# Full and 64-row matmuls chosen piece by piece in a fused attention and FFN kernel, with a new order of TensorE's work

## The chip, the cores and the metric

The kernel runs on one core of a Trainium2 chip. The core has a matrix engine (TensorE, PE in the profile; its weight loads stand as PEld), three engines for elementwise work (VectorE or DVE, ScalarE or ACT, GpSimd or POOL), and SyncE (SP), which here only issues DMA transfers. The metric is the device time of one execution in microseconds, lower being better. The time before is 522.56 us, the median of three runs between 522.38 and 522.78 us.

## The reference

Attention with mixed heads, and behind it a feed-forward network with a squared ReLU:

```python
scores = scale * np.matmul(q, k.transpose(0, 1, 3, 2))        # (8, 12, 448, 448)
scores = np.einsum('bhij,hg->bgij', scores, w_pre)            # heads mixed
attn = np.exp(scores - np.max(scores, axis=-1, keepdims=True))
attn = attn / (np.sum(attn, axis=-1, keepdims=True) + 1e-09)
attn = np.einsum('bhij,hg->bgij', attn, w_post)               # heads mixed again
attn_out = np.matmul(attn, v)                                 # (8, 12, 448, 64)
x = attn_out.transpose(0, 2, 1, 3).reshape(3584, 768)
h = np.maximum(x @ w_in, 0.0)                                 # w_in (768, 2048)
out = h * h @ w_out                                           # w_out (2048, 768)
```

There are 8 batches, 12 heads, 448 positions and a head size of 64. Inputs and output are float32; the products run in bfloat16.

## The kernel before

Work is cut into units, each a short run of matmuls on TensorE. For each batch there are these kinds:

- `tr` (L718): q and k are transposed, 28 small matmuls a unit.
- `qk` (L864): the scores of two heads (or of four half tiles) for a tile of up to 128 query rows. ACT or DVE evicts the result from PSUM to the buffer `stage`, which has two slots, one per query tile. SP then issues relays: DMA transfers that move ten query rows of all heads at a time from `stage` to the ring `dring` (L910). A tile's evictions wait until the relays of the tile two before it have landed.
- `dir` (L815): for the first 22 chunks of batch 0 the scores are made without that relay.
- `pre` (L933): two chunks of ten rows are mixed over heads. ACT takes the exponential and the row sums (L950), DVE the reciprocal (L964), and POOL (DVE in the first chunks) scales the mixing weights and a rest of the exponentials with it (L971, L986).
- `post` (L1016, L1031): the second mixing, fourteen matmuls of 60 columns for two chunks, evicted to `a2t` in two halves.
- `av` (L1097): the product with v, evicted to `xt`, the FFN's input in transposed form.
- `h` (L1148, L1176): the FFN's first product. The 2048 inner features are 16 blocks of 128; a block needs six steps of 128 input features. In batches 0, 1 and 7 a block covers half of the batch's positions (220 or 228), otherwise all 448.
- `o` (L1242, L1293): the second product, for a tile of 128 positions and two halves of 384 output columns, sixteen steps each. Evictions go to `osb`, and POOL issues two stores for each tile (L1325).

A block of the first product is evicted with a ReLU on ACT or DVE (L1204, L1205) and squared on DVE (L1214).

The first product exists in two forms. The full form uses all 128 rows of the array: six matmuls a block (`emit_F1_full`, L1148, used for batches 0 and 1). The other uses 64-row tiles: two blocks are made together, every step is cut into two matmuls of 64 rows that run side by side in the upper and the lower half of the array, each for another block and into another PSUM bank; then the halves change places (`emit_F1`, L1176). A pair of blocks is two units of twelve matmuls, and both blocks are finished only at the end of the second. The second product is in 64-row tiles too (`emit_F2`, L1293), each of its four units sixteen matmuls, save for the last two tiles of the last batch (`emit_last`, L1242).

All eight PSUM banks are handed out by a planner, which walks through a model of the kernel when the program is built. Ten streams hold the units in their own sequence: 0 `tr`, 1 `qk`, 2 `pre`, 3 `post`, 4 `av`, 5 `dir`, 6 and 7 `h`, 8 and 9 `o`. A string of digits, `ORDER`, says from which stream TensorE takes its next unit. For the other engines the planner takes what its model has ready first, and a `FLEX` task goes to ACT or DVE, whichever would end it sooner in the model. So TensorE's order is written out, and the order on the other engines, the waits and the banks follow from it through the planner's costs. A unit whose bank is still to be evicted waits, and on every engine what is behind a waiting instruction waits too.

## Time and profile before

| what | value |
|---|---|
| time, median of three runs | 522.56 us (522.38 to 522.78) |
| profiled execution, first to last instruction | 522.5 us |
| PE busy | 508.7 us, 97%, 9,477 matmuls |
| ACT busy | 432.9 us, 83% |
| DVE busy | 402.8 us, 77% |
| POOL busy | 264.7 us, 51% |
| DMA moved | 72.36 MB, mean 138 GB/s |

No other time of the profiled execution is listed than its span; the median of the runs lies 0.06 us above it. The profile comes as a page with busy times, strips of 40 slices and groups of instructions, and as answers to questions: tables by stage, the chain of work that ended last (followed back from the last instruction to what released it), the waits, and the instructions in order of time. In such a row a number in square brackets is the idle time of the engine just before, with what ended it.

### The profile page before, as it was taken

Reading aid. Unit: us, or ns where it says so; the run is one execution under the profiler, and the core shown is the slowest. Engines: PE = TensorE matmul, PEld = TensorE weight load, DVE = VectorE, ACT = ScalarE, POOL = GpSimd, SP = SyncE. Lnnn points to the kernel's source line nnn. Section 1 sums busy time; section 2 is a strip of 40 time slices with the busy share of each in tenths; the row PEclk is TensorE's granted clock in tenths of the full one; section 3 lists DMA queues with packets and bytes.
Section 4 is the critical chain, followed back from the end, with each engine's and each line's share of the span. In section 5 each row is a group of like instructions: output and inputs, shape, how many; then the busy total and the mean of one; then the engine's idle time right before and its main releaser. Section 6 shows DMA issues by size and latency. Waiting matters only on the chain.

```text
span 522.5 us, 23103 instructions
## 1 busy us (share of the span) xinstructions
PE 508.7 (97%) x9477; PEld 320.4 (61%) x9477; DVE 402.8 (77%) x1038; ACT 432.9 (83%) x1243; POOL 264.7 (51%) x571
## 2 busy tenths in 40 slices
PE   8999999899989999999999999999999999999997
PEld 3455677567757665557546665566555665568874
DVE  8988878779969879977798868986797857955440
ACT  4899989889989889988998898999788899867421
POOL 9926556534753477335672486435654354243000
PEclk9999999999999999999999999999999999999999
DMA  8999989945995489646994689537985557451013
GB/s 113 194 228 181 215 166 182 191 93 114 170 192 131 108 163 180 146 94 155 177 183 86 138 174 191 125 70 159 175 141 114 132 129 136 85 128 53 3 24 99
DMA packets 83024, 72.36 MB, mean 138 GB/s; under 512 B 7160, under 2 KB 80424, under 8 KB 82920
## 3 DMA queue, kind: packets, MB, share of 16 engines
q0 software_dynamic: 37632, 33.83, 39.8%
q1 hardware_dynamic: 45000, 36.86, 29.2%
q8 instruction: 76, 1.25, 1.0%
q14 instruction: 28, 0.23, 0.1%
q10 hardware_dynamic: 288, 0.20, 0.1%
HBM read 47.27 MB, written 11.01 MB: 112 GB/s over the span
## 4 chain that ended last, share of the span: by engine, by line
PE 81%; DVE 7%; ACT 5%; DMA 5%; issue 1%; POOL 0%; SPq 0%; DVEq 0%
PE ps L1293 25%; PE ps L1176 18%; PE ps L933 6%; PE ps L1016 6%; PE ps L1097 6%; PE ps L864 5%; PE ps L815 5%; DMA dring<-stage 5%; PE ps L1148 4%; ACT pring L950 3%; DVE stage L479 2%; PE ps L1242 2%; PE ps L718 2%; PE ps L591 1%; DVE qkt L479 1%
## 5 line engine op out<-in xcount | busy, mean ns | idle before, releaser
L950 ACT ACTIVATE pring<-ps 128x448 bf16<-128x448 f32 x360 | 192.0, 560 | 12.9 <-PE ps L933 11.8
L1293 PE MATMUL ps<-w_out_sb,h2t 64*128 64x384 bf16 x1664 | 151.6, 323 | 2.3 <-issue 1.7
L971 POOL TENSOR_TENSOR wk2s<-wk2b,rinv 128x120 bf16<-128x120 bf16 (+1 forms) x179 | 70.5, 394 | 142.3 <-DVE rinv L964 141.2
L479 DVE CAST a2t<-ps 128x420 bf16<-128x420 f32 (+1 forms) x202 | 122.2, 640 | 15.5 <-PE ps L1031 14.4
L1176 PE MATMUL ps<-xt,w_in_sb 64*128 64x448 bf16 (+2 forms) x1344 | 120.7, 323 | 0.1
L478 ACT ACTIVATE stage<-ps 128x448 bf16<-128x448 f32 (+1 forms) x195 | 101.2, 556 | 14.9 <-PE ps L864 11.9
L478 ACT ACTIVATE a2t<-ps 128x420 bf16<-128x420 f32 (+1 forms) x166 | 99.7, 655 | 15.5 <-PE ps L1031 15.3
L479 DVE CAST stage<-ps 128x448 bf16<-128x448 f32 (+1 forms) x165 | 98.9, 615 | 16.8 <-PE ps L864 13.0
L1293 PEld LDWEIGHTS ps<-w_out_sb,h2t 64*128 64x128 bf16 x1664 | 77.5, 94 | 52.0 <-issue 4.0
L1176 PEld LDWEIGHTS ps<-xt,w_in_sb 64*128 64x128 bf16 x1344 | 61.7, 94 | 40.0 <-PE ps L933 2.0
L1325 POOL DMA_DIRECT2D out_dram<-osb x52 | 33.6, 652 | 100.8 <-ACT pring L950 39.6
L950 ACT ACTIVATION_READ_ACCUMULATOR pring<-ps 128x1 f32 x360 | 81.2, 226 | 0.0
L986 POOL TENSOR_TENSOR ptail<-pring,rinv 128x128 bf16<-128x128 bf16 x171 | 70.2, 411 | 0.0
L1016 PEld LDWEIGHTS ps<-wk2s,pring 60*128 60x128 bf16 x2160 | 47.7, 94 | 25.9 <-DVE stage L479 2.3
L1205 DVE TENSOR_SCALAR h1t<-ps 128x448 bf16<-128x448 f32 (+2 forms) x99 | 46.9, 482 | 14.4 <-PE ps L1176 11.3
L1016 PE MATMUL ps<-wk2s,pring 60*128 60x60 bf16 x2160 | 55.1, 187 | 2.3 <-DVE stage L479 1.1
L1214 DVE TENSOR_TENSOR h2t<-h1t 128x448 bf16<-128x448 bf16 (+2 forms) x176 | 55.5, 345 | 2.1 <-ACT h1t L1204 1.5
L933 PE MATMUL ps<-dring,wk 64*64 64x448 bf16 (+1 forms) x676 | 52.6, 363 | 1.4 <-ACT stage L478 0.8
L964 DVE RECIPROCAL rinv<-rowsum 128x2 f32<-128x2 f32 (+1 forms) x184 | 29.0, 157 | 31.5 <-ACT pring L950 30.7
L864 PE MATMUL ps<-qkt 64*128 64x448 bf16 (+1 forms) x360 | 50.3, 353 | 1.5 <-DVE stage L479 0.6
L1204 ACT ACTIVATE h1t<-ps 128x448 bf16<-128x448 f32 (+2 forms) x77 | 35.0, 461 | 14.4 <-PE ps L1176 12.6
L1097 PEld LDWEIGHTS ps<-a2t,vraw 128*64 128x64 bf16 x960 | 38.5, 109 | 6.0 <-ACT osb L478 2.4
(60 smaller groups left out, 536.8 us busy)
## 6 DMA issues: line engine op xcount, KB each, us to landing
dring<-stage SPq DMA_DIRECT2D x309, 105.0 KB
out_dram<-osb POOLq DMA_DIRECT2D x52, 192.0 KB, 3.9
vraw<-in_v_dram POOLq DMA_DIRECT2D x48, 128.0 KB
qraw<-in_q_dram POOLq DMA_DIRECT2D x48, 112.0 KB, 5.2
kraw<-in_k_dram POOLq DMA_DIRECT2D x48, 112.0 KB, 4.9
w_in_sb<-in_moe_w_in_dram POOLq DMA_DIRECT2D x8, 384.0 KB, 19.6
w_out_sb<-in_moe_w_out_dram POOLq DMA_DIRECT2D x8, 384.0 KB, 16.0
dring<-stage SPq DMA_DIRECT2D x30, 42.0 KB
```

Of the source, the lines that this page charges most:

```text
L478: return eng.activation(o, i_, AF.Copy)
L479: return eng.tensor_copy(o, i_)
L864: r_ = eng.matmul(ps[y * w:(y + 1) * w, g.banks[x], 0:S], qkt[r0:r0 + 64, pb, p + y, 0, i0:i0 + w], qkt[r0:r0 + 64, pb, p + y, 1, :], star ...
L933: r_ = eng.matmul(ps[64 * y:64 * y + 64, gr.banks[x], 0:S], wk1[64 * x:64 * x + 64 - R0 * x, :], dring[64 * x:64 * x + 64 - R0 * x, (g0 + ...
L950: return eng.activation(pring[:, pr, 0:S], ps[:, gr.banks[x], 0:S], AF.Exp, accum_out=rowsum[:, pr, :])
L971: return eng.tensor_tensor(wk2s[:, p0:p0 + n, :], i0.to_broadcast([128, n, PR]), rinv[:, p0:p0 + n, :].to_broadcast([128, n, PR]), ALU.mult)
L986: return eng.tensor_tensor(ptail[:, p0 // 2, :, :], pring[:, p0:p0 + 2, 0:PJ], rinv[:, p0:p0 + 2, :].to_broadcast([128, 2, PJ]), ALU.mult)
L1016: r_ = eng.matmul(ps[:, gr.banks[x], o0:o0 + PR], pring[64 * x:64 * x + PR, pr + y, (2 * k + 1) * PJ:(2 * k + 3) * PJ], wk2s[64 * x:64 * x ...
L1097: r_ = eng.matmul(po, vraw[:, h, sl, :], m, start=(k == 0), stop=(k == NS))
L1176: r_ = eng.matmul(ps[:, g.banks[x], 0:n], w_in_sb[64 * y:64 * y + 64, ft, t * 128:(t + 1) * 128], xt[64 * y:64 * y + 64, ft, c0:c1], start ...
L1214: return eng.tensor_tensor(h2t[:, t16, o0:o0 + n], h1t[:, s, 0:n], h1t[:, s, 0:n], ALU.mult)
L1293: r_ = eng.matmul(ps[:, g.banks[hh], 0:FH], h2t[64 * y:64 * y + 64, t16, col:col + 128], w_out_sb[64 * y:64 * y + 64, t16, hh * FH:(hh + 1 ...
```

## The change

Both products get a flag for each piece. `F1_FULL` has one digit for each of the 88 pairs of blocks: 16 each for batches 0, 1 and 7, 8 each for batches 2 to 6. `F2_FULL` has one for each of 32 places (four to a batch; tiles count from 0). A pair with a 1 is made in the full form: two units of six matmuls, each with a bank of its own, so that the first block can be evicted while the second is made. With a 0 it is made in 64-row tiles as before. A tile of the second product with a 1 has its two halves made one after the other in full matmuls. The one string `ORDER` is replaced by another; it differs from the 38th unit on. Batches 0 and 1 stay full, which they were. Beyond them 9 pairs become full in batches 3, 4 and 5 (two, two and five), 14 of the 16 pairs of batch 7, and its tiles 0 and 1.

```diff
 ORDER = (
-    "0011055055105510551555511155555553115550013555555553135002555555335555335531002555112551"
+    "0011055055105510551555511155555553315555150031555551355555020555533553355522003555111551"
...
 )
+F1_FULL = "1111111111111111111111111111111100000000000001010000001100101111000000001011111011111111"
+F2_FULL = "00000000000000000000000000001100"
...
-        def emit_F1(b, parts, t16, s_F):
+        def emit_F1(b, parts, t16, s_F, full):
             c0, c1 = cols_of(parts[0])[0], cols_of(parts[-1])[1]
             n = c1 - c0
-            g = _Group(2)
-            before = None
+            gs = [_Group(1), _Group(1)] if full else [_Group(2)]
+            ins = ([t for part in parts for t in xtev[(b, part)]]
+                   + w_of[(0, t16 * NWP // NFFT)])
+            ths = []
             for ph in range(2):
                 def fn_h(eng, en, ph=ph):
                     r_ = None
                     for ft in range(NFT):
+                        if full:
+                            t = t16 + ph
+                            r_ = eng.matmul(ps[:, gs[ph].banks[0], 0:n],
+                                            w_in_sb[:, ft, t * 128:(t + 1) * 128],
+                                            xt[:, ft, c0:c1],
+                                            start=(ft == 0), stop=(ft == NFT - 1))
+                            continue
                         for y in range(2):
...
+                before = [] if full else ths[:]
+                t_h = unit(s_F, "h%d_%d_%d_%d" % (b, c0, t16, ph), fn_h, ins + before,
+                           NFT * (n / 2.4 + (2.5 if full else 4.3)), "full" if full else "row",
+                           gs[ph] if full else gs[0], NFT if full else 2 * NFT)
+                t_h.sync = before
+                ths.append(t_h)
...
             for x in range(2):
-                after_F1(b, parts, t16 + x, t_h, c0, n, g, x)
+                after_F1(b, parts, t16 + x, ths[x if full else 1], c0, n,
+                         gs[x] if full else gs[0], 0 if full else x)
...
-            g = _Group(2)
+            full = F2_FULL[4 * b + tile] == "1"
+            gs = [_Group(1), _Group(1)] if full else [_Group(2)]
...
                         for t16 in range(q0, q0 + nk):
+                            if full:
+                                r_ = eng.matmul(
+                                    ps[:, gs[ph].banks[0], 0:FH],
+                                    h2t[:, t16, col:col + 128],
+                                    w_out_sb[:, t16, ph * FH:(ph + 1) * FH],
+                                    start=(t16 == 0), stop=(t16 == NFFT - 1))
+                                continue
...
                 for t16 in range(0, NFFT, 2):
-                    if b < 2:
-                        for t in range(2):
-                            emit_F1_full(b, parts, t16 + t, s_F1[t16 // 2 % 2])
-                    else:
-                        emit_F1(b, parts, t16, s_F1[t16 // 2 % 2])
+                    emit_F1(b, parts, t16, s_F1[t16 // 2 % 2], F1_FULL[n_f] == "1")
+                    n_f += 1
```

How the change moves instructions is shown at three places, in rows that give line, operation, operands, shape and count. Lines of the changed kernel stand two or more higher or lower than those before.

Place A is on PE, at about 56 us of the profile before: the scores (`qk`, written to `ps` from `qkt`) of batch 1's second query tile, between blocks of batch 0's first product (`ps<-xt,w_in_sb`) and the last `pre` units of batch 0 (`ps<-dring,wk`). Before:

```order
L864 MATMUL ps<-qkt 128x448 x4
L1148 MATMUL ps<-xt,w_in_sb 128x220 x12
L864 MATMUL ps<-qkt 128x448 x2
L1016 MATMUL ps<-wk2s,pring 128x60 x12
L1031 MATMUL ps<-wk2b,ptail 128x60 x2
L864 MATMUL ps<-qkt 128x448 x2
L1148 MATMUL ps<-xt,w_in_sb 128x220 x12
L933 MATMUL ps<-dring,wk 64x448 x10
```

The same place now:

```order
L935 MATMUL ps<-dring,wk 64x448 x8
L1155 MATMUL ps<-xt,w_in_sb 128x220 x12
L935 MATMUL ps<-dring,wk 64x448 x2
L1018 MATMUL ps<-wk2s,pring 128x60 x12
L1033 MATMUL ps<-wk2b,ptail 128x60 x2
L1018 MATMUL ps<-wk2s,pring 128x60 x12
L1033 MATMUL ps<-wk2b,ptail 128x60 x2
L1155 MATMUL ps<-xt,w_in_sb 128x220 x12
L866 MATMUL ps<-qkt 128x448 x4
```

The last `pre` units of batch 0 stood behind four of this tile's six `qk` units; now they, and blocks and `post` units with them, stand ahead of the first.

Place B is on DVE, at about 73 to 78 us of the profile before: evictions of the third query tile's scores to `stage`, between the squares of the first product (`h2t<-h1t`). Before:

```order
L1205 TENSOR_SCALAR h1t<-ps 128x220
L1214 TENSOR_TENSOR h2t<-h1t 128x220
L964 RECIPROCAL rinv<-rowsum 128x2
L1214 TENSOR_TENSOR h2t<-h1t 128x228
L479 CAST stage<-ps 128x448
L1214 TENSOR_TENSOR h2t<-h1t 128x228 x2
L479 CAST stage<-ps 128x448
```

The same place now:

```order
L481 CAST a2t<-ps 128x84x5
L1202 TENSOR_TENSOR h2t<-h1t 128x220
L481 CAST stage<-ps 128x448 x2
L1193 TENSOR_SCALAR h1t<-ps 128x228
L1202 TENSOR_TENSOR h2t<-h1t 128x220
L1202 TENSOR_TENSOR h2t<-h1t 128x228 x2
L481 CAST stage<-ps 128x448 x2
```

The first two evictions to `stage` stood apart, the first behind a square of the 228-column part; now the two stand together, ahead of that part's first ReLU.

Place C is on DVE, at about 96 to 100 us of the profile before: the first output tile's eviction (`osb<-ps`) among reciprocals and evictions to `a2t` and `stage`. Before:

```order
L964 RECIPROCAL rinv<-rowsum 128x2
L479 CAST stage<-ps 64x448 x2
L964 RECIPROCAL rinv<-rowsum 128x2
L479 COPY osb<-ps 128x2x192 x2
L964 RECIPROCAL rinv<-rowsum 128x2
L479 CAST a2t<-ps 128x84x5
L964 RECIPROCAL rinv<-rowsum 128x2
```

The same place on DVE now:

```order
L481 CAST a2t<-ps 128x84x5 x3
L481 COPY osb<-ps 128x2x192
L481 CAST stage<-ps 64x448 x3
L966 RECIPROCAL rinv<-rowsum 128x2
L481 CAST stage<-ps 64x448
L966 RECIPROCAL rinv<-rowsum 128x2
```

And on ACT, where the other half is evicted now:

```order
L952 ACTIVATE pring,rowsum<-ps 128x448 x4
L480 ACTIVATE a2t<-ps 128x84x5 x3
L480 ACTIVATE osb<-ps 128x2x192
L480 ACTIVATE stage<-ps 64x448
L952 ACTIVATE pring,rowsum<-ps 128x448 x4
```

DVE copied both halves of the tile ahead of a reciprocal; now each of the two engines copies one.

77 lines of the change are left out of this document (28 added, 49 removed).

## The prediction

> **What bounds the kernel now.** First the page: the span, the busy shares, and the strip of DMA shares in 40 slices of 13.06 us.
>
> ```profile
> span 522.5 us, 23103 instructions
> ...
> PE 508.7 (97%) x9477; PEld 320.4 (61%) x9477; DVE 402.8 (77%) x1038; ACT 432.9 (83%) x1243; POOL 264.7 (51%) x571
> ...
> DMA  8999989945995489646994689537985557451013
> ```
>
> PE is busy in 508.7 of 522.5 us, so at most 13.8 us of the span are visibly PE's waits, start and end included. The first eight digits of the DMA strip are 8 or 9: until about 104 us transfers run nearly without a pause, and there a wait can end with a transfer whatever PE does. Next the table by stages, which says where PE stands still (columns: stretch, its length, then each engine's busy time, PE first).
>
> ```profile
> 52.00:78.00 26.00, 24.18 (x425) 18.57 (x420) 21.34 (x70) 23.18 (x74) 14.57 (x33) 1.00 1.05 191
> 78.00:104.00 26.00, 24.22 (x456) 16.63 (x458) 20.65 (x56) 23.20 (x69) 16.40 (x35) 1.00 0.97 189
> 104.00:130.00 26.00, 26.00 (x520) 18.58 (x516) 22.08 (x62) 23.84 (x67) 10.07 (x25) 1.00 0.46 102
> 130.00:156.00 26.00, 24.26 (x534) 16.97 (x533) 21.20 (x68) 23.32 (x71) 17.47 (x37) 1.00 0.95 179
> 156.00:182.00 26.00, 25.62 (x488) 17.80 (x488) 22.80 (x57) 23.50 (x70) 10.61 (x26) 1.00 0.54 122
> ```
>
> Idle PE: 1.82, 1.78, 0, 1.74 and 0.38 us. So three stretches hold 5.34 us that another order could win back, each with the DMA share near 1; elsewhere TensorE is the bound, and there only cheaper TensorE work helps. The granted clock is 1.00 throughout. The sum is made against the profiled span, 522.5 us; the median of the runs, 522.56, lies 0.06 above it, and I treat the two as one.
>
> **The price of the two forms.** The chain of work that ended last, over the whole run, gives what a piece costs until the next one starts (start, length, engine and line, matmuls).
>
> ```profile
> 26.64 4.65 PE ps L815 x24
> ...
> 84.67 2.46 PE ps L1148 x24
> ...
> 145.85 1.41 PE ps L1293 x16
> ...
> 147.64 1.30 PE ps L1293 x16
> ...
> 250.68 1.14 PE ps L1176 x12
> ...
> 492.60 9.36 PE ps L1176 x192
> 501.95 6.50 PE ps L1293 x80
> 508.45 10.52 PE ps L1242 x64
> ```
>
> L1293 stands with 1.41 and with 1.30 us for the same sixteen matmuls: the dearer ones are followed by work in another tile shape. A change of shape costs 0.11 us. With that taken off the ends: a block of 228 columns in 64-row tiles is 9.36 / 16 = 0.585 us, a full one (2.46 - 0.11) / 4 = 0.59. At 448 columns the 64-row unit is 1.14 us, and six full matmuls, by L815, which has the same shape, 6 x (4.65 - 0.11) / 24 = 1.135. In the second product two 64-row matmuls are 2 x 6.50 / 80 = 0.163 us, one full one 10.52 / 64 = 0.164.
>
> The flags turn 9 pairs of batches 3 to 5 full, 14 of the last batch's 16, and two tiles of the second product. Pairs: 18 blocks x (1.135 - 1.14) + 28 x (0.59 - 0.585) = +0.05 us; tiles: 64 x 0.0015 = +0.1 us. **Form: +0.2 us**, ends -0.1 and +0.5; it is on the path, since TensorE is the bound there. TensorE issues 340 matmuls fewer (9477 to 9137) and as many weight loads fewer, which these steps already contain.
>
> Changes of shape, counted along the order over full, 64-row, 64-column and 64 x 64 work: 263 before, 263 after (64-row to 64 x 64 and back falls from 135 to 106, full to either and back rises to make up for it). **Shape changes: 0.** So the mix of forms as such pays nothing, and what is left is the order.
>
> A rule speaks against the full form, and the row for it is this one:
>
> ```profile
> L1293 PEld LDWEIGHTS ps<-w_out_sb,h2t 64*128 64x128 bf16 x1664 | 77.5, 94 | 52.0 <-issue 4.0
> ```
>
> A weight load takes 94 ns. The Trainium skill, page "TensorE: Matmul & The Clock Gate", section "Part 3: Packing small matmuls", says that a weight load overlaps running matmuls only when it goes to other rows of the array; full matmuls, which use all rows, would then show theirs. By that rule the change would cost 340 x 0.094 = 32 us, against 0.2 by the rows. The trace disagrees: a full matmul of 384 columns at L1242 takes 0.164 us, and the 64-row pair 0.163.
>
> **The order, place by place.** Place A, the scores' evictions of batch 1's second query tile. The stage buffer has two slots, and this tile needs the one that the tile before it leaves only when its relays have landed.
>
> ```profile
> 48.59 10.25 DMA dring<-stage
> ...
> 56.41 0.79 PE L864 MATMUL ps<-qkt 64*128 64x448 bf16 x4
> ...
> 58.86 1.85 ACT L478 ACTIVATE stage<-ps 128x448 bf16<-128x448 f32 x4 [0.98 <-DMA dring<-stage]
> 58.86 0.62 DVE L479 CAST stage<-ps 128x448 bf16<-128x448 f32 x1 [1.18 <-DMA dring<-stage]
> ...
> 59.54 0.34 PE L1016 MATMUL ps<-wk2s,pring 60*128 60x60 bf16 x12 [0.81 <-DVE stage L479]
> ```
>
> The matmuls run at 56.41, the slot comes free at 48.59 + 10.25 = 58.84, both eviction engines stand behind it, and PE, out of banks, waits 0.81 us. The new order puts six blocks of the first product (6 x 0.59), four post units and three pre units ahead of these matmuls, at least 4.3 us (a post unit is 0.20 us, rows at D). They then run from 60.7, after 58.84; even if the chain of relays starts 1.3 us later, because the pre unit that opens it has moved back by so much, 60.1 is early enough. **A: -0.8 us**, ends -0.8 and 0.
>
> Place B is the same wait one tile later.
>
> ```profile
> 63.61 13.37 DMA dring<-stage
> ...
> 73.09 0.35 PE L864 MATMUL ps<-qkt 64*128 64x448 bf16 x2
> ...
> 77.00 0.54 ACT L478 ACTIVATE stage<-ps 128x448 bf16<-128x448 f32 x1 [0.99 <-DMA dring<-stage]
> ...
> 77.60 0.38 PE L933 MATMUL ps<-dring,wk 64*64 64x448 bf16 x4 [0.79 <-ACT stage L478]
> ```
>
> The slot is free at 76.98. Before, one scores unit ran at 73.09 and the next 3 us later; now both stand together, their four evictions stand early on both eviction engines, and only three blocks (1.8 us) follow before the next pre unit wants two banks. If the chain of relays moves with the pre units that open it (2.2 us earlier by the order), the slot is free at 74.8 and the wait goes: -0.8. If the DMA queues set its end, 77.0 stays, PE stops about 2.2 us before it instead of 0.8: +1.4. **B: +0.3**, the middle, since the DMA share of 1.05 speaks for a fixed end and the earlier pre units against it.
>
> Place C, behind the first output tile.
>
> ```profile
> 97.52 1.02 DVE L479 COPY osb<-ps 128x384 f32<-128x384 f32 x2
> ...
> 98.55 0.17 DVE L964 RECIPROCAL rinv<-rowsum 128x2 f32<-128x2 f32 x1
> ...
> 98.84 0.69 POOL L1325 DMA_DIRECT2D out_dram<-osb  x1 [0.45 <-DVE rinv L964]
> ...
> 99.74 0.64 POOL L1325 DMA_DIRECT2D out_dram<-osb  x1 [0.21 <-issue]
> ...
> 101.20 0.34 PE L1016 MATMUL ps<-wk2s,pring 60*128 60x60 bf16 x12 [0.47 <-POOL ptail L986]
> ...
> 102.41 0.38 PE L933 MATMUL ps<-dring,wk 64*64 64x448 bf16 x4 [0.31 <-DVE a2t L479]
> ...
> 103.65 0.38 PE L864 MATMUL ps<-qkt 64*64 64x448 bf16 x4 [0.64 <-DVE stage L479]
> ```
>
> VectorE copies both halves of the tile, POOL issues the two stores and only then scales the weights that PE's next post unit needs: 0.47 us, and behind it 0.31 and 0.64 of piled-up evictions, 1.42 in all. The new order gives one half to ScalarE (0.5 us instead of 1.02 on VectorE) and runs the next transposes two units earlier, so that their evictions are out of the pile. The two stores still stand ahead of the scaling on POOL, 1.33 us. **C: -0.7**, half of it, ends -1.42 and 0.
>
> Place D.
>
> ```profile
> 149.34 0.17 PE ps L1016 x12
> 149.50 0.03 PE ps L1031 x2
> 149.53 0.16 PE ps L1293 x2
> 149.69 1.74 issue
> ```
>
> PE stops inside a run of sixteen matmuls, with no semaphore to wait for, right behind three post units. I read this as instructions that came late: the page's instruction queue is read in 76 packets.
>
> ```profile
> q8 instruction: 76, 1.25, 1.0%
> ```
>
> With 18,954 matmuls and weight loads that is one packet per 249 of PE's instructions; 680 fewer make 2.7 packets fewer, and all later packets begin elsewhere. The one long stop in 76 packets needs a coincidence that the new order hardly repeats at this spot. But a post unit is 28 instructions in 0.20 us, and runs of three post units rise from 5 to 16. **D: -0.9**, half, ends -1.74 and, at one stop per five such runs, +3.5.
>
> Sum: 0.2 + 0 - 0.8 + 0.3 - 0.7 - 0.9 = -1.9; 522.5 - 1.9 = 520.6 us.
>
> **Rivals.** (1) The waits only move: the order is new from the 38th unit to the end, and evictions keep ACT at 83% and DVE at 77%, so what A, C and D lose returns at places that I can't name. For it: counted along both orders, units that stand close behind the work whose eviction they need are about as many now as before. Against it: two of the five stretches above show that 26 us can pass with 0 to 0.4 us idle. Time 522.5.
>
> (2) Slower by late instructions: at the rate of place D, one stop in five runs of three post units, 16 runs give three stops, 5.2 us instead of 1.74: +3.5, and with the other terms (-1.0) 525.0. It decides from two stops on. Against it: four of the five runs went by without one, and 73 packets leave fewer chances than 76.
>
> (3) Slower by place B: the slot stays closed until 77.0, A's gain is spent waiting there (+0.8), PE waits 1.4 longer, and C's pile forms behind the late batch (0 instead of -0.7); D's gain stays: 522.5 + 0.2 + 1.4 - 0.9 + 0.5 for the four evictions to be worked off = 523.7. It decides if the slot opens after about 76.
>
> (4) The exposed weight loads of the rule above: 554.5.
>
> **How the numbers follow.** Forecast 520.6: 0.47. Rival 1: 0.20. Rival 2: 0.20. Rival 3: 0.12. Rival 4: 0.01, as the trace contradicts it. Repeated runs of this kernel spread by 0.4 us, and 0.2% or 1.05 us is about what can be told from no change. So faster 0.47, same 0.20, slower 0.33. The best case has all of A to D gone: 0.2 - 0.8 - 0.8 - 1.42 - 1.74 = -4.6, 517.9. I let the range start at 518.2 and end at rival 2's 525.0, which leaves a little under 2 in 10 outside; the forecast's own range is 518.2 to 521.5.
>
> **What would show it.** Form: at the end, blocks of 228 columns at 0.58 to 0.60 us in the full form; weight loads exposed would read 0.68. A: no wait of stage evictions for relays near 60 us. B: the wait near 77 us, under or over 0.8 us. C: PE's waits behind the first output tile under 1 us. D: "issue" in PE's waits at 0 or at several times 1.7 us. The prediction is wrong if the three stretches still hold 5 us of idle PE or if later ones, now at 0 to 0.4, reach 1 us.

## The result

The changed kernel takes 525.81 us (median of 20 runs, 524.07 to 527.51), the kernel before beside it 522.38 us (20 runs, 521.14 to 527.06). The medians are 3.4 us apart. The ratio is 1.0053, its 95% interval 1.0035 to 1.0071, or 1.8 to 3.7 us; it lies below the ratio of the medians, 1.0066, since a few executions of the kernel before are long. The forecast was 520.6 us and its range ended at 525.0: the time lies outside the range, and on the other side of no change. The prediction took 0.4 us, the spread of its three runs, for that of the kernel; over 20 runs it is 5.9 us.

The page of the changed kernel, with the lines that answer to those of before:

```profile
span 524.8 us, 22429 instructions
...
PE 510.0 (97%) x9137; PEld 320.6 (61%) x9137; DVE 403.5 (77%) x1045; ACT 434.9 (83%) x1236; POOL 266.6 (51%) x571
...
DMA  8999999746894479656983589647894468441003
...
q8 instruction: 73, 1.20, 0.9%
```

TensorE is visibly idle for 14.8 us instead of 13.8, and three packets fewer bring its instructions. The stages, in the same stretches (stretch, length, then the busy time of each engine, PE first):

```profile
52.00:78.00 26.00, 24.09 (x406) 17.58 (x401) 21.14 (x71) 23.82 (x77) 16.01 (x35) 1.00 1.06 192
78.00:104.00 26.00, 24.32 (x471) 16.89 (x470) 20.49 (x57) 23.33 (x66) 15.24 (x33) 1.00 0.91 180
104.00:130.00 26.00, 25.69 (x506) 17.99 (x504) 20.50 (x55) 22.34 (x71) 10.12 (x24) 1.00 0.49 106
130.00:156.00 26.00, 25.09 (x552) 18.06 (x543) 22.52 (x67) 24.80 (x75) 18.27 (x39) 1.00 0.93 174
156.00:182.00 26.00, 24.53 (x494) 17.04 (x481) 20.52 (x52) 21.52 (x62) 10.44 (x25) 1.00 0.50 116
234.00:260.00 26.00, 24.61 (x486) 16.29 (x484) 21.45 (x57) 21.78 (x63) 16.46 (x36) 1.00 0.79 160
```

PE's idle time is 1.91, 1.68, 0.31, 0.91, 1.47 and, in a last stretch in which PE was busy for all 26.00 us before, 1.39 us. The last two show the sign of being wrong that the prediction had named: later stretches that reach 1 us. The first two stretches hold as much as before, though the waits in them are others. The old waits behind the scores of the second query tile (place A) and behind the first output tile (place C) are gone or small:

```profile
61.54 0.55 PE L866 MATMUL ps<-qkt 64*128 64x448 bf16 x4
62.09 0.29 PE L1018 MATMUL ps<-wk2s,pring 60*128 60x60 bf16 x8
...
101.15 0.34 PE L1018 MATMUL ps<-wk2s,pring 60*128 60x60 bf16 x12
...
103.25 0.38 PE L935 MATMUL ps<-dring,wk 64*64 64x448 bf16 x4 [0.23 <-ACT stage L480]
```

In their place stand waits that the order before did not have. I call the new places E, F and G. Place B, and E, the same thing with the first scores of the fourth query tile, which the new order runs about 5 us of TensorE's work earlier (relay chain, ACT and PE rows):

```profile
61.90 13.51 DMA dring<-stage
...
75.44 0.54 ACT L480 ACTIVATE stage<-ps 128x448 bf16<-128x448 f32 x1 [1.91 <-DMA dring<-stage]
...
76.03 0.38 PE L935 MATMUL ps<-dring,wk 64*64 64x448 bf16 x4 [1.02 <-ACT stage L480]
76.65 0.38 PE L935 MATMUL ps<-dring,wk 64*64 64x448 bf16 x4 [0.23 <-DVE stage L481]
...
81.30 11.32 DMA dring<-stage
...
93.50 1.10 ACT L480 ACTIVATE stage<-ps 64x448 bf16<-64x448 f32 x2 [1.47 <-DMA dring<-stage]
...
94.83 0.38 PE L935 MATMUL ps<-dring,wk 64*64 64x448 bf16 x4 [1.18 <-DVE stage L481]
```

At B the stage's slot opens at 75.41 us, 1.57 us earlier than before, but the scores were made earlier still, and PE waits 1.25 us instead of 0.79. At E the scores stand ready, the slot opens at 92.62, ACT has stood behind it for 1.47 us, and PE, out of banks, for 1.18.

F is a wait for a load of K; G is in batch 3, behind the stores of an output tile on POOL's queue:

```profile
161.72 0.41 PE L720 MATMUL ps<-ident,kraw 64*64 64x64 bf16 x28 [1.42 <-DMA kraw<-in_k_dram]
...
247.91 1.28 POOL L1327 DMA_DIRECT2D out_dram<-osb  x2 [3.78 <-ACT pring L952]
249.18 0.42 POOL L973 TENSOR_TENSOR wk2s<-wk2b,rinv 128x120 bf16<-128x120 bf16 x1
249.53 0.43 POOL L988 TENSOR_TENSOR ptail<-pring,rinv 128x128 bf16<-128x128 bf16 x1
249.88 0.64 POOL L624 DMA_DIRECT2D kraw<-in_k_dram  x1
250.50 0.65 POOL L635 DMA_DIRECT2D vraw<-in_v_dram  x1
252.22 0.61 POOL L635 DMA_DIRECT2D vraw<-in_v_dram  x1 [1.06 <-issue]
252.84 0.40 POOL L973 TENSOR_TENSOR wk2s<-wk2b,rinv 128x120 bf16<-128x120 bf16 x1
253.19 0.40 POOL L988 TENSOR_TENSOR ptail<-pring,rinv 128x128 bf16<-128x128 bf16 x1
...
253.70 0.34 PE L1018 MATMUL ps<-wk2s,pring 60*128 60x60 bf16 x12 [1.33 <-ACT a2t L480]
```

POOL issues two stores, a load of K, a load of V, stops for 1.06 us with nothing that the profile names, issues a second load of V, and only then scales what PE's next post unit needs. The row of PE names an eviction; but PE starts 0.11 us after POOL's `ptail` at 253.19 has ended. I take it that without POOL's stop of 1.06 us both would have been as much earlier.

### The profile page after: what moved, and what is told of

Its sections match the earlier page's. It is cut to its first block, busy times and chain, and to the rows that moved or that the text cites. A ratio compares the mean times of both kernels' runs of the same rounds, so it can differ in the third digit from the quotient of the medians.

```text
span 524.8 us, 22429 instructions
## 1 busy us (share of the span) xinstructions
PE 510.0 (97%) x9137; PEld 320.6 (61%) x9137; DVE 403.5 (77%) x1045; ACT 434.9 (83%) x1236; POOL 266.6 (51%) x571
## 4 chain that ended last, share of the span: by engine, by line
PE 78%; DMA 7%; ACT 7%; DVE 4%; POOL 1%; issue 1%; SPq 0%; DVEq 0%; POOLq 0%
PE ps L1290 22%; PE ps L1163 12%; PE ps L1155 9%; PE ps L935 6%; DMA dring<-stage 6%; PE ps L1099 6%; PE ps L866 5%; PE ps L1018 5%; ACT pring L952 5%; PE ps L817 4%; PE ps L1282 2%; PE ps L1230 2%; PE ps L720 2%; DVE stage L481 1%; ACT a2t L480 1%; DMA kraw<-in_k_dram 1%
## 5 line engine op out<-in xcount | busy, mean ns | idle before, releaser
L1290 PE MATMUL ps<-w_out_sb,h2t 64*128 64x384 bf16 x1536 | 140.2, 323 | 0.0
L481 DVE CAST a2t<-ps 128x420 bf16<-128x420 f32 x194 | 115.5, 641 | 15.1 <-PE ps L1033 14.7
L481 DVE CAST stage<-ps 128x448 bf16<-128x448 f32 (+1 forms) x175 | 104.6, 616 | 16.7 <-PE ps L866 9.2
L480 ACT ACTIVATE a2t<-ps 128x420 bf16<-128x420 f32 x174 | 101.9, 657 | 14.4 <-PE ps L1033 13.7
L480 ACT ACTIVATE stage<-ps 128x448 bf16<-128x448 f32 (+1 forms) x185 | 96.4, 559 | 18.6 <-PE ps L866 14.1
L1290 PEld LDWEIGHTS ps<-w_out_sb,h2t 64*128 64x128 bf16 x1536 | 71.5, 94 | 45.1 <-issue 1.2
L1327 POOL DMA_DIRECT2D out_dram<-osb x52 | 33.5, 649 | 103.1 <-ACT pring L952 41.0
L1163 PE MATMUL ps<-xt,w_in_sb 64*128 64x448 bf16 (+1 forms) x792 | 82.0, 344 | 0.2
L1155 PE MATMUL ps<-xt,w_in_sb 128*128 128x220 bf16 (+2 forms) x660 | 80.7, 275 | 0.5 <-ACT a2t L480 0.2
L1155 PEld LDWEIGHTS ps<-xt,w_in_sb 128*128 128x128 bf16 x660 | 60.3, 98 | 15.6 <-ACT h1t L1192 1.8
L1163 PEld LDWEIGHTS ps<-xt,w_in_sb 64*128 64x128 bf16 x792 | 35.7, 94 | 31.2 <-PE ps L935 2.4
```

Of the source, the lines that this page charges most:

```text
L480: return eng.activation(o, i_, AF.Copy)
L481: return eng.tensor_copy(o, i_)
L1155: r_ = eng.matmul(ps[:, gs[ph].banks[0], 0:n], w_in_sb[:, ft, t * 128:(t + 1) * 128], xt[:, ft, c0:c1], start=(ft == 0), stop=(ft == NFT - 1))
L1163: r_ = eng.matmul(ps[:, gs[0].banks[x], 0:n], w_in_sb[64 * y:64 * y + 64, ft, t * 128:(t + 1) * 128], xt[64 * y:64 * y + 64, ft, c0:c1], s ...
L1290: r_ = eng.matmul(ps[:, gs[0].banks[hh], 0:FH], h2t[64 * y:64 * y + 64, t16, col:col + 128], w_out_sb[64 * y:64 * y + 64, t16, hh * FH:(hh ...
```

## The experiments

A profiled run's time was 1.7 to 1.8 us above its span in all of them (526.61 with 524.8, 541.04 with 539.3), so spans of different runs can be set beside each other. Single executions of one kernel spread over 3 us and more; most conclusions therefore rest on medians of 5 or more runs, and of a profile mainly on rows that recur.

The first four ran with one set of runs of before, 522.69 us. Below, a unit's number counts the digits of `ORDER`; by that count the two orders part at the 35th. Only some of the changed lines are shown, and `...` stands for the others.

**The new order with the old forms** (run e1).

```diff
-F1_FULL = "1111111111111111111111111111111100000000000001010000001100101111000000001011111011111111"
-F2_FULL = "00000000000000000000000000001100"
+F1_FULL = "1111111111111111111111111111111100000000000000000000000000000000000000000000000000000000"
+F2_FULL = "00000000000000000000000000000000"
```

> The new order with the forms of before (batches 0 and 1 full, all else in 64-row tiles save the last two output tiles). Theory O (the order costs: waits on relays, on a load of k and on POOL that the new order brings, about 4 us less what it saves): the loss stays, 524.5 to 526.5 us against 522.4 before; the waits near 76, 94 and 161 us are there as in the changed kernel. Theory F (the full pieces cost): the loss goes, 522 to 523 us. Changes of shape fall from 263 to 258, which is worth 0.5 us.

Measured: 541.68 us, ratio 1.0376 (1.0354 to 1.0399). Both theories missed by 15 us and more. The loss stands in batch 5 and at the end: by the starts of the same `pre` units, this run falls about 9 us behind the changed kernel between 341 and 400 us of the latter, and another 3 us after 479 us. These are the stretches of batch 5 (the changed kernel has 0, 0.08 and 0 us of idle PE in them):

```profile
338.00:364.00 26.00, 24.17 (x502) 14.84 (x502) 18.07 (x44) 20.15 (x55) 9.43 (x23) 1.00 0.40 88
364.00:390.00 26.00, 23.84 (x456) 13.90 (x450) 16.59 (x40) 21.33 (x61) 15.63 (x32) 0.93 0.90 164
390.00:416.00 26.00, 22.85 (x418) 12.04 (x417) 19.31 (x47) 20.73 (x60) 10.56 (x25) 1.00 0.49 97
```

The new order puts up to nine other units, 4 us of work, between the two units of a pair that is full. In the 64-row form such a pair holds two banks all that time and releases both blocks only at its end. I take this from the code as the cause; no run varies the banks alone. The granted clock fell to 0.93 in the middle stretch (24 matmuls of the first product took 4.25 us at 381.72, against 2.44 at 399.87), which is a part of the loss too. So order and form belong together: the new order was made for pairs that release their first block early, and neither may be judged with the other's partner.

**The order before with the new forms** (e2).

```diff
 ORDER = (
-    "0011055055105510551555511155555553315555150031555551355555020555533553355522003555111551"
...
+    "0011055055105510551555511155555553115550013555555553135002555555335555335531002555112551"
...
 )
```

> The old order with the new forms. Without an order made for them the full pieces bring 29 more changes of shape (292 against 263). Theory O: 29 x 0.11 us = 3.2 us and nothing else, so 525 to 526 us, with no new wait before batch 3 (up to about 230 us the trace is that of before). Theory F: more than that, 3.2 us and the 3.4 us of the changed kernel, 528 to 530 us.

Measured: 526.04 us, ratio 1.0068 (1.0045 to 1.0092), as theory O had it, to 0.1 us. Counted along the order, the forms raise the changes of shape from 263 to 292 here. At 0.094 us each, that is 2.7 of the 3.35 us. This price is the difference, in the traces, between a piece that is followed by another shape and one that is not: sixteen matmuls of the second product, 1.394 against 1.301 us.

**All pairs and tiles full, in the order before** (d), the dose to that price.

```diff
-F1_FULL = "1111111111111111111111111111111100000000000001010000001100101111000000001011111011111111"
+F1_FULL = "1111111111111111111111111111111111111111111111111111111111111111111111111111111111111111"
-F2_FULL = "00000000000000000000000000001100"
+F2_FULL = "11111111111111111111111111111111"
```

(and `ORDER` as before)

> The order of before with every pair of the first product and every tile of the second in the full form: a dose for the price of the form. 488 shape changes in place of 263. My prediction's 0.11 us for one: 225 x 0.11 = 24.8 us more, 547; the 0.094 us that the traces give for one: 543.7; and about 800 instructions fewer for TensorE, no gain from that by either. If a full pair were cheaper in itself than a 64-row pair by more than 0.03 us, the time would come out under 541.

Measured: 540.77 us (two executions) beside 523.53, ratio 1.0338 (1.0306 to 1.0371), so 17.2 us for 225 more changes, 0.077 each, below both figures expected. The pieces themselves cost the same: counted at 0.094 us, the changes of shape take 45.9 us instead of 24.7, and what is left of PE's idle time is 26.3 instead of 29.8 us. A pair in full form sets its first block free early and holds one bank at a time; that this is what saves the 3.5 us of waits is likely, but not shown. The kernel also has 3,008 matmuls and weight loads fewer, not about 800 as I had expected.

**Which part of the order.** Four kernels take one order up to a unit and the other from there; the forms of a pair go with the order that it stands in (e3 has the new ones throughout).

The order before for 337 units (169 us), then the new one (e3):

```diff
...
-    "2224443117633002276711181227762383338221836720110766662020772238338338111812291193193339"
+    "2244433276113177300226761116722833833382128002672117667020367223833831181812291193193339"
```

> The old order for the first 337 units, to about 169 us (both orders have done the same units there), then the new order, with the new forms. By the two traces the changed kernel is 0.7 us behind at that point and 2.3 us at the end. Theory O: the late part's loss alone, +1.6 us, 523.5 to 524.5 us, with the relay wait near 94 us and the wait for k near 161 us gone and the 1.3 us wait near 253 us still there. A theory that the loss is all early: 522.4.

Measured: 525.62 us, ratio 1.0065 (1.0042 to 1.0088): nearly the whole loss, higher than expected. Place G stands in its profile too, with a stop of POOL of 1.33 us. The reverse (h1):

```diff
-    "2224443117633002276711181227762383338221836720110766662020772238338338111812291193193339"
+    "2224443117633002276711181227762383338221836720110766662020772238338338111118122442293391"
...
-F1_FULL = "1111111111111111111111111111111100000000000001010000001100101111000000001011111011111111"
+F1_FULL = "1111111111111111111111111111111100000000000000000000000000000000000000000000000000000000"
-F2_FULL = "00000000000000000000000000001100"
+F2_FULL = "00000000000000000000000000000000"
```

> The new order for the first 337 units (to about 169 us), the order and forms of before from there. Theory W (the loss is the sum of the waits in the traces): up to there the new order loses 0.7 us against the profiled execution of before, 2.4 against one without the stop at 149.7 us, so 523.3 to 525.1. Theory L (the loss lies after 240 us, since the run with the old order first and the new one behind lost 2.9 us already): within 0.6 us of before, 522.1 to 523.3.

Measured: 523.84 us beside 522.72, ratio 1.0020 (0.9988 to 1.0051): +1.1 us with an interval of -0.6 to +2.7. The median lies in the range of theory W, but the interval takes in that of theory L too. By the medians most of the loss is in the second half; the interval of e3, 2.2 to 4.6 us, overlaps with this one. Two later seams were to narrow it down:

```diff
...
-    "8113811932293391393124224422183118138333822244422163361711171633360202721763361227721002"
+    "1822289111933391139222244383183318113822244442236116317137116233360202721763361227721002"
```

> The order of before for the first 502 units (to about 257 us), the new order and forms from there, so without the new order of tiles and loads around 249 to 254 us. Theory L (the loss sits around 249 to 264 us): the run comes within 0.6 us of before, 522.1 to 523.3, against 525.6 with the new order from 169 us on. The rival, that the new order loses in small pieces all through its second half: half of the 2.9 us stays, 524.0 to 524.6.

```diff
...
-    "2227600226733373612167337212672200762200911913939181183318133822244422181138333831422442"
+    "7200263363722176313637237212672200762200911913939181183318133822244422181138333831422442"
...
-F1_FULL = "1111111111111111111111111111111100000000000001010000001100101111000000001011111011111111"
+F1_FULL = "1111111111111111111111111111111100000000000000000000001100101111000000001011111011111111"
```

> The order and forms of before for the first 639 units (to about 327 us), the new ones from there. It leaves out the loads and tails around 249 to 264 us, where the changed kernel waited 1.5 to 2.5 us. Theory G (the second half loses there): 522.2 to 523.4. Rival F (the second half loses by stops at the ends of instruction blocks at 317 to 382 us, seen with 1.3 to 1.7 us in three of the four profiles that have the new order there): 523.8 to 525.

Measured: 526.00 us beside 522.72 (1.0064, 1.0039 to 1.0090), over both ranges expected, and 524.86 beside 523.53 (1.0051, 1.0020 to 1.0082), in the range of rival F; but of stops like place D its profile has only one of 0.25 us behind 317 us. Neither seam is clean: right behind the seam each has a long wait of a post unit for POOL's scaling, which neither whole order has there (a row of PE from each run, h2 first):

```profile
256.11 0.34 PE L1018 MATMUL ps<-wk2s,pring 60*128 60x60 bf16 x12 [1.94 <-POOL ptail L988]
```

```profile
330.60 0.34 PE L1018 MATMUL ps<-wk2s,pring 60*128 60x60 bf16 x12 [2.29 <-POOL ptail L988]
```

With that wait taken off in full, h3 would be 1.0 us under the kernel before that ran beside it (524.86 - 2.29 = 522.57, an estimate), and h2 1.3 us above (524.06). The granted clock was also lower in many of these executions, 0.993 to 0.997 in 7 of 12 of h2 and 5 of 9 of h3, against 3 of 35 and 2 of 20 of the kernel before beside them. So these two runs don't settle where after 257 us the rest is lost.

**Four places repaired** (e4): the changed kernel with five units moved to later places, two at B, one each at E, F and G.

```diff
-    "3113332244243223663332672277233761131661117623367222444731176622176133367227763313677137"
-    "6672129920029333912281383238422440206711820081118131811383226671362137722263676133673337"
-    "2224443117633002276711181227762383338221836720110766662020772238338338111812291193193339"
+    "3113332244243223663332672277233761131661117623367222444737616221176133367227763313677137"
+    "6672299200293331912281383238422440206711820081118131811383226671362137722263676133673337"
+    "2224443117633002276711181227762383338221836720110766662027702238338338111812291193193339"
...
-    "8113811932293391393124224422183118138333822244422163361711171633360202721763361227721002"
+    "8113811932293391393124224422183118138333822244422163631711171633360202721763361227721002"
```

> The changed kernel with five units moved a little later, at its four largest new waits: the third query tile's first two scores units of batch 1 (near 72 us), the fourth tile's first (near 90 us), the transposes of k near 160 us, and one post unit near 252 us. Theory O: the waits of 1.25, 1.18, 1.42 and 1.33 us shrink to under 0.5 us each, 3 us less, 522 to 523.5 us. Theory that these waits are set by work that comes late whatever TensorE does, so that the time is spent at the next place: 525 to 526 us.

Measured: 524.24 us, ratio 1.0038 (1.0026 to 1.0051), between the two ranges expected. By the medians 1.6 us of the loss is gone; the interval overlaps with that of the changed kernel (1.0035 to 1.0071). That is about half of what the waits promised, and other waits stand in the trace: at E 0.43 us remain, behind G two waits of 0.31 and 0.53 us appear at the next post units, and POOL still stops for 1.06 us before the second load of V.

**The early half with B and E repaired** (r), and the order before from unit 337 on.

```diff
-    "3113332244243223663332672277233761131661117623367222444731176622176133367227763313677137"
+    "3113332244243223663332672277233761131661117623367222444737616221176133367227763313677137"
...
-    "6672129920029333912281383238422440206711820081118131811383226671362137722263676133673337"
+    "6672299200293331912281383238422440206711820081118131811383226671362137722263676133673337"
...
-    "2224443117633002276711181227762383338221836720110766662020772238338338111812291193193339"
+    "2224443117633002276711181227762383338221836720110766662020772238338338111118122442293391"
...
```

> The new order for the first 337 units, with two units of the third query tile and the first of the fourth moved to later places (as in the run with four moves), then the order and forms of before. If place A and the rest of the early reordering are worth what the trace of before had them at (0.8) and the new waits at 75 and 93 us cost what the trace shows (0.5 and 1.2), the run comes to 521.4 to 522.6, before or a little under it; if the early reordering has no worth of its own, it stays at 523.3 to 524.2 with the run that had the new order there unmoved.

Measured: 523.20 us beside 523.00, ratio 1.0016 (0.9997 to 1.0036), between the two expectations. In its profile the waits at A and C are gone or small, and those at B and E are down to 0.54 and 0.43 us; the time is still not shown to be below before.

**Both kernels a second time under the profiler** (b_again and a_again, programs unchanged).

> The order and the forms of the kernel before, on a second execution under the profiler. Theory S (the 1.74 us stop at 149.7 us belonged to that one profiled execution, whose time was about 1.8 us over the median): the stop is absent or under 0.5 us, the span is 520.3 to 521.5. Theory T (the stop is in every execution of this order): it is there again with 1.5 us or more, and the span is near 522.4. The waits of places A (0.81), B (0.79) and C (0.38 and 0.34) recur within 0.3 us under both.

> The changed kernel on a second execution under the profiler, to see which waits belong to its order. Theory W (the waits that the first trace showed are the order's own): place B 1.0 to 1.5 us in all, the fourth query tile's wait near 93.5 us 1.2 to 1.7, the wait for the raw K load near 161.7 us about 1.4, POOL's late scaling near 253.7 us about 1.3 recur within 0.4 us each. Theory N (they are accidents of one execution): half of them or more are under 0.4 us.

Measured: 523.24 beside 522.72, ratio 0.9995 (0.9968 to 1.0022), span 521.5; and 527.04, ratio 1.0065 (1.0033 to 1.0098), span 527.2. Theory S holds for place D: behind the same three post units sixteen matmuls now run without a stop.

```profile
147.93 0.33 PE L1018 MATMUL ps<-wk2s,pring 60*128 60x60 bf16 x12
148.09 0.19 PE L1033 MATMUL ps<-wk2b,ptail 60*128 60x60 bf16 x2
148.12 1.47 PE L1290 MATMUL ps<-w_out_sb,h2t 64*128 64x384 bf16 x16
```

B (0.79) and C (0.47, 0.30, 0.64) recurred to 0.01 us; A came with 0.39 instead of 0.81. (In nine of the ten profiles with this early order A lies between 0.35 and 1.42; in d it is absent.) In the changed kernel B (1.23), E (1.27) and G (1.33) recurred, F did not. But the second execution has four stops of another kind, in the chain of work that ended last:

```profile
317.93 0.19 PE ps L1163
318.12 0.96 issue
...
370.86 0.38 PE ps L1163 x4
371.24 1.36 issue
372.60 0.91 PE ps L1163 x7
```

The other two stand at 156.4 (0.88) and 163.0 us (0.70). The trace holds a record of each packet of the instruction queue. Set beside PE's stops (from the start of the last matmul to that of the next; all times in us, the last column is the place of the waiting instruction in its block of 256):

```
kernel      PE last, next     16 KB packet, start and end   end to next   place
before      149.37  151.43    148.94  149.83                1.60          193
b_again     187.88  188.78    186.00  187.72                1.06          193
after        54.99   55.45     53.12   54.06                1.39          193
a_again     156.19  157.33    154.78  155.67                1.66          193
a_again     162.69  163.71    161.52  162.45                1.26          193
a_again     317.77  319.08    316.66  317.61                1.47          193
a_again     370.89  372.60    370.30  371.23                1.37          193
e3          380.74  382.30    379.88  380.76                1.54          193
```

All of them stand at the same place of a block, counted over the instructions that the trace records, and each ends 1.1 to 1.7 us behind a packet. These packets had begun 4.1 to 5.6 us after PE passed that place of the block before, against medians of 1.2 to 1.5 us for all packets of a profile, and PE mostly needs 5 to 9 us for a block. (In e3 the waiting instruction is a wait for a semaphore; it starts at 382.30, and the next matmul at 382.52.) So this shows that the stops are late instructions, as read at place D. The Trainium skill, page "Runtime: NRT & Kernel Launch", section "Instruction fetch mechanics", says that instructions come in blocks of 256 through a DMA queue and that crossing a block's end is mostly hidden. The blocks agree with the trace; hidden they are for all but none to five of some 75 packets, and these cost up to 5.8 us in one execution.

**Every instruction moved 70 places** (s_after, s_before): a longer first warm-up, so that the block boundaries fall into other units.

```diff
-                for _ in range(n):
-                    r_ = eng.matmul(ps[0:128, g.banks[0], 0:S], warm[:, 0:128], warm[:, :],
+                cols = [S] + [8] * 48 if now < 6000.0 and n > 10 else [S] * n
+                for w in cols:
+                    r_ = eng.matmul(ps[0:128, g.banks[0], 0:w], warm[:, 0:128], warm[:, 0:w],
                                     start=True, stop=True)
```

> The changed kernel with the first warm-up unit made of 49 matmuls (one of 448 columns, 48 of 8) in place of 14 of 448, so that every later instruction of TensorE stands 70 places further on in the program. What it computes is untouched. Theory F (stops without a semaphore come where TensorE reaches the end of a block of 256 instructions and the next 16 KB packet of instructions has landed late): the stop of 0.46 to 1.02 us in the unit post32 near 55 us is no longer there, any stop without a semaphore stands at other units, but again at the same place of a block of 256, 1.0 to 1.7 us behind the end of a packet; the median moves by up to 1.5 us either way from 525.8. Rival (the stop belongs to the unit, post32, whatever its place in the program): it is there again with 0.4 us or more.

> The kernel before with the same longer warm-up, 70 places further on. Theory F: stops without a semaphore at other units than those of its two profiles (149.4, 187.4 us), the median within 1.0 us of before. If the whole loss of the changed kernel came from where its blocks end, shifting both would bring the two together within 1 us; if it comes from its waits, the changed one stays 2 to 3.5 us longer.

Measured: 527.08 us (1.0078, 1.0057 to 1.0098) and 524.84 us (1.0045, 1.0018 to 1.0072), beside 523.53. The stop in post32, near 55 us, which had stood in the two profiles of the changed kernel and in e4, is gone. (It is not the new order's own: with the order before, the runs e2, d, c_before and t_before have a stop at the same place, of 0.59, 1.08, 0.59 and 0.58 us.) The new ones in the shifted changed kernel are in the middle of a pre unit, at 53.8 us (lines stand one further here), and at 111.5 and 206.0, all again at place 193, 1.4 to 1.6 us behind a packet; the shifted kernel before had none:

```profile
53.68 0.49 PE ps L936 x5
54.17 1.61 issue
55.79 0.38 PE ps L936 x3
```

So they belong to a place in the block, not to post units. By the medians the shift did not bring the two kernels together: 2.2 us stay between them, within what was expected if the waits cost as well, though the intervals of the two ratios overlap. The shifted kernel before missed its own expectation: it is 1.3 us above before, not within 1.0, and no run shows why. (Behind its first stop the changed one also shows a granted clock under 1 for one slice, 0.995 over the span.)

Three profiles of each kernel, by starts of PE's units (us; "own work" is each unit's usual distance to the next, "shape changes" is their number, 263, at 0.094, "stops" those of the table's kind, "rest" all other idle time, the start included; 6.4 to 6.5 us of each span stand in no column):

```
profile     span    own work   shape changes   stops   rest
before      522.5   460.5      24.7            2.1     28.8
b_again     521.5   460.5      24.7            0.9     28.9
s_before    521.9   460.2      24.7            0.0     30.5
after       524.8   459.8      24.7            0.7     33.1
a_again     527.2   460.0      24.7            5.8     30.3
s_after     526.2   459.8      24.7            3.8     31.5
```

On the mean the changed kernel is 4.1 us longer in these six: 0.5 less own work, 2.2 more of waits, 2.4 more of stops. The split of the last two is weak, with stops between 0.7 and 5.8 us in executions of much the same program. In the runs below they differ less: c_after has 2.1 us of stops and c_before 1.2, t_after 2.2 and t_before 1.8. So it is not shown that the new order has more of them.

**Three quarters of the output stores' bytes left out** (c_after, c_before), to see what the traffic on POOL's queue does. Each store that POOL issues writes one of its four groups of columns; the others are never written.

```diff
-                    dst = bass.AP(out.tensor, row * F, [[NT * F, 64], [OP, 4], [1, OP]])
-                    eng.dma_start(dst, osb[p0:p0 + 64, :, s, :]).then_inc(
+                    dst = bass.AP(out.tensor, row * F, [[NT * F, 64], [OP, 1], [1, OP]])
+                    eng.dma_start(dst, osb[p0:p0 + 64, 0:1, s, :]).then_inc(
```

> The changed kernel with the 48 stores of output tiles on POOL's queue cut to a quarter of their columns, so that three quarters of those outputs are not written; TensorE, the relays and the loads keep their places. Theory F (the stops at the ends of instruction blocks come from packets held up by the bursts of POOL's queue): they fall under 1.0 us in all (0.7, 5.8 and 3.8 in three profiles), the 16 KB packets that start over 3 us late from 11 to 15 down to 8 or fewer, and the time falls by 1 to 3 us, to 523 to 525. Rival (the stops don't hang on that traffic): time and stops stay, 525 to 527.

> The same cut in the kernel before. Theory F: it had only 2.1, 0.9 and 0.0 us of such stops, so it gains less than the changed kernel, 0.3 to 1.3 us, to 521.2 to 522.4; what is left between the two, 1.5 to 2.5 us, is the share of the waits. Rival: both gain alike, and 3 to 3.5 us stay between them.

Measured: 522.76 us (0.9995, 0.9974 to 1.0017) and 521.63 us (0.9981, 0.9956 to 1.0007), beside 523.00. Without these bytes the changed kernel is about 3 us shorter and the other 1.4, and 1.1 us stay between them instead of 3.4. At place G POOL no longer stops, and PE does not wait:

```profile
245.88 0.66 POOL L624 DMA_DIRECT2D kraw<-in_k_dram  x1
246.53 1.28 POOL L635 DMA_DIRECT2D vraw<-in_v_dram  x2
247.79 0.43 POOL L973 TENSOR_TENSOR wk2s<-wk2b,rinv 128x120 bf16<-128x120 bf16 x1
...
248.67 0.34 PE L1018 MATMUL ps<-wk2s,pring 60*128 60x60 bf16 x12
```

So at G the stop goes away with the stores' bytes. But these alone don't decide whether POOL stops: in c_before, with the same small stores, POOL stops for 1.62 us at another load of V, behind two stores, a load of K and a load of V (first row), and at 320 us the changed kernel issues two full stores and three loads of V without a pause (the other two):

```profile
306.05 0.61 POOL L635 DMA_DIRECT2D vraw<-in_v_dram  x1 [1.62 <-issue]
```

```profile
319.55 1.32 POOL L1327 DMA_DIRECT2D out_dram<-osb  x2 [2.47 <-ACT a2t L480]
320.85 1.90 POOL L635 DMA_DIRECT2D vraw<-in_v_dram  x3
```

What makes POOL stop stays open. The part of theory F on late instructions missed: the profile of c_after still has stops of 0.75, 0.33 and 0.99 us, and 10 packets that begin over 3 us late, about as many as with all stores (11, 12 and 15); c_before has 12. What holds these packets up is not settled by this run.

**The stores issued by SP** (t_after, t_before), all bytes kept.

```diff
-            t_od = plan.add("odma%d_%d" % (b, tile), POOL, fn_od, evs,
-                            {POOL: (580.0 * 2, 0.0)}, b * 1000.0 + 710,
+            t_od = plan.add("odma%d_%d" % (b, tile), SP, fn_od, evs,
+                            {SP: (600.0 * 2, 0.0)}, b * 1000.0 + 710,
```

> The changed kernel with the stores of the output tiles issued by SP in place of POOL; all outputs are written. Theory P (the stores' places on POOL's queue cost: POOL's stop of 1.06 us before a load of V near 251 us, and the wait of 1.3 to 1.5 behind it): that stop is gone, the time falls by 1 to 3 us, 523 to 525. Rival R (SP's relays stand behind the stores now): waits for the relays grow, over 527. Rival B (the bytes cost, whatever the queue): 525 to 527.

> The same for the kernel before. Theory P: its POOL did not stop there, so it gains 0 to 1.4 us (the cut of the stores gained it 1.4), 521.2 to 523. Rival R: over 524. A time under 521.5 would make it a faster kernel than both.

Measured: 537.70 us (1.0280, 1.0266 to 1.0294) and 534.15 us (1.0221, 1.0204 to 1.0238), beside 522.88. Rival R, far over its bound. SP's own waits in the changed kernel tell why (total, times, longest):

```profile
SPq L1327 <- ACT h1t L1192: 16.8, 1, 16.8
...
SPq L1407 <- ACT osb L480: 14.9, 5, 7.5
...
SPq L1327 <- ACT osb L480: 14.6, 1, 14.6
```

L1327 is the store: SP stood at single stores for 16.8 and 14.6 us, with the relays behind them in its queue. POOL's stop at G is not there either. Whether it is the stores' bytes or their place on POOL's queue that costs the changed kernel its 3 us stays open.

## Why the prediction was wrong

The step that failed is the one that made a sum of the old waits alone. Waits that the new order would bring were put at nothing, without a search for them, and two of them, E and G, outweigh what A and C gained.

- **What the sum lacked: new waits.** I searched four places where the order before waited and none where the new one would. E is the mechanism of B one tile later: 1.18, 1.27 and 0.68 us in the three profiles of the changed kernel. G is akin to the mechanism that I had named at C, transfers ahead of the scaling on POOL's queue (here loads of K and V behind two stores), at another output tile: 1.33 in all three, and with it a stop of POOL that no row of before shows. F came with 1.42, 0 and 0.28. This is rival 1, that the waits only move, and it was priced wrongly, at exactly nothing.
- **The base of the sum** failed too: "the median of the runs, 522.56, lies 0.06 above it, and I treat the two as one". The profiled runs of the study are 1.7 to 1.8 us longer than their spans, so the profiled execution, of 522.5 us of span, was one of about 524.3 (an estimate from that difference), 1.7 longer than the median.
- **D, -0.9.** The reading (late instructions) was right. The gain was not: the 1.74 us belonged to that one execution and were not in the median from which they were taken off. Without D the same sum gives 522.5 - 1.0 = 521.5.
- **Form, +0.2.** Small, as worked out; the table has 0.5 us less of own work. In the last batch blocks in full form take 9.36 / 16 = 0.585 us, to the digit what the 64-row form took (the chain, at the end):

```profile
494.90 1.41 PE ps L1282 x8
496.31 9.36 PE ps L1155 x96
505.67 2.60 PE ps L1282 x16
```

- **Shape changes, 0.** Right: 263 in either kernel. The price of one was a little high, 0.11 against 0.094 from the traces and 0.077 net in the dose.
- **A, -0.8.** The wait is gone, as worked out (the scores at 61.54, after the slot). What it was worth varies with the execution, 0.81 and 0.39 us in the two profiles of before.
- **B, +0.3.** Measured +0.46 by the first two profiles of each (1.25 and 1.23 against 0.79); the number was luck, as the middle of -0.8 and +1.4. The slot opened at 75.4, between the two ends that I had set, 74.8 and 77.0. In the shifted kernel, behind the stop at 53.8 us, the wait is not there.
- **C, -0.7.** Too small: 1.42 us became 0.23, so -1.2.
- **Rival 2** came nearest in time, 525.0, and its mechanism took part: two of the three profiles of the changed kernel have 3.8 and 5.8 us of late instructions, where it said 5.2. Its condition was wrong: the stops don't follow runs of three post units. They stand at one place of a block and fell into pairs of the first product, output tiles and pre units as well. Rival 3 did not happen (the slot moved with the pre units), nor rival 4 (0.585 us per block, not 0.68).

By the rows of the first profiles, D (0.9), A (0.4, against 0.39), B (0.2), C (-0.5), E (1.2) and G (1.3) add up to 3.5 of the 5.2 us between forecast and time. This is an estimate, since e4 shows that taking waits away gives back only about half of them. The other 1.7 us stay open. F and late instructions can hold them, but F did not recur, and that the new order has more late instructions is not shown: it has 11 to 15 packets that begin over 3 us late against 7 to 9 before, in three profiles each, but the order before has 12 and 10 in c_before and t_before, and e4 has 9.

## What to carry to other kernels

Take the sum against an execution whose time is known to be typical, or profile twice: a stop without a semaphore that is in one trace may not be in the next. Where an order is new, the places to search are those where a unit now stands closer behind a relay, a load or another engine's scaling than it did, and not only those where the old order waited. An order that splits pairs of blocks needs the form that releases its bank early, and that form needs an order that keeps changes of shape few, so changing one without the other (here +19 and +3.4 us) says little about the pair.

## What the hardware showed that I had not expected

- TensorE stopped at one place in a block of 256 instructions when the next 16 KB packet had begun late (2.5 to 5.6 us after it passed that place of the block before), and went on 1.1 to 1.7 us after the packet's end. A stop was 0.25 to 2.06 us from start to start, the sum over one execution 0 to 5.8 us.
- At place G POOL stood 1.05 to 1.33 us before a second load of V, with two stores and two loads issued in the 4.6 us before it, in all six profiles that have the new order there and full stores on POOL, and not with quarter stores or with the stores on SP. Elsewhere the same kinds of transfers went by without a stop, and c_before has one of 1.62 us; the condition is not known.
- A change of the tile shape on TensorE cost 0.094 us between otherwise equal pieces (1.394 against 1.301), and full and 64-row matmuls, each with its weight load, took the same time per unit of work (0.585 us for a block of 228 columns in either form).
